# RetNet and mixture of depths in one kernel: the first batch's ranking, stores, loads and weights in another order

## The chip, the core and the metric

The kernel runs on one NeuronCore of a Trainium2 chip. The metric is the device time of one execution in microseconds (us). A core has a matrix engine (PE), a vector engine (DVE), a scalar engine (ACT), a general engine (POOL) and a queue processor (SP) that only issues transfers here; 16 DMA engines move data between memory and the on-chip SBUF. PE writes its results to PSUM.

## The reference

```
ret = ((q @ k^T) / 8 * gamma_h^(i-j) for j <= i) @ v     # 8 batches, 8 heads, 576 tokens, 64 wide
x = ret as (batch, 576, 512)
scores = x @ w_gate                                      # one number per token
top = the 128 tokens of a batch with the highest scores
out = x;  out[top] = x[top] + sigmoid(scores[top]) * (relu(x[top] @ w1) @ w2)   # w1 512x1024
```

Everything is float32. A token's rank in its batch is the number of tokens that score higher; tokens with rank below 128 go through the MLP.

## The kernel before, in words

A batch of 576 tokens is cut into 9 chunks of 64. A step of the main loop (line 487) handles two chunks, so there are 36 steps for 8 batches, and one more to finish; step 4 holds the last chunk of batch 0 and the first of batch 1. For each step one load of 1 MB brings q, k, v and a second layout of k (`load`, L108). POOL scales v with the decay (`scaled`, L189, tile `vs`). PE makes the products of q and k (`sc_ps`), the running state (`u_ps`, copied to `st` by ACT, L209), and, one step later, the output (`y_ps`). DVE applies the causal mask (`masked`, L262). `values` scales the output by the other decay: in the steps in `BUSY` by eight small ACT instructions (L272), in the others by one of DVE (L275); then two DVE instructions score the two chunks (L283). `stored` (L291 to L296) writes the output of a step in two transfers, or four where a step spans two batches.

When a batch, or a part of it (`cuts`), is scored, four functions rank it: `flatten` lays the scores on a diagonal, `spread` broadcasts them over the partitions by a matmul and an ACT copy, `compare` counts on DVE how many scores are higher than those of one block of 128 tokens (with a first instruction that picks the block's own scores), `one_hot` turns ranks into a selection. `fetch` makes token indices by a matmul and starts an indirect gather of 128 rows from memory on POOL (L375); the rows must have been stored before. `mlp` transposes them on PE (`turn`, tile `xg_ps`, L394) and puts eight parts into a list: four `up` (first layer, `h_ps`) and four `down` (second layer, `ye_ps`), 1.9 us of PE each. Each step takes some parts from the list so that they are used up by the next batch's turn. After the last `down`, POOL scatters the new rows (L419).

The order on each engine in `ENGINES` is the order in which the code emits instructions; POOL isn't in that set before, so a scheduler orders it. PE executes the matmuls of a step in an interleave of two streams; the plan `inner` puts a function at a place (step, i) inside it, `first` right after the matmuls, `soon` and `mid` after `values`, `late` and `then` at the step's end. Transfers are issued by SP in order. `pe` counts PE work and, about once a step, issues a due weight piece (a list `weights` with due steps) and the next load, both made to wait behind a matmul of that step. Each transfer also waits until the one eight places earlier on SP has landed.

```
load(); load()                        # start: table, loads 0 and 1, w_gate halves,
load(); load(); ...; load()           # loads 2 and 3, second table part, load 4
weights.append((5 + f // 2, ...))     # w1 pieces due in steps 5 to 8, w2 pieces in 9 to 12
```

Of the kernel before, what the change touches and what calls it, by code (L numbers as in the profile page):

```python
# [10 lines left out]
F32 = mybir.dt.float32  # L11
# [6 lines left out]
P = 128  # L18
# [3 lines left out]
BEFORE = 65  # L22
SURE = 8
ET = mybir.EngineType
ENGINES = {ET.PE, ET.DVE, ET.Activation, ET.SP}


def layout(NC, HG, cap):
# [11 lines left out]
def kernel(  # L40
# [22 lines left out]

    nc = tc.nc
    NS = qkvk.shape[0]
    DM = w1.shape[0]
    F = w1.shape[1]
    D = DM // H
    KD, FB = DM // P, F // P
    B = len(outs)  # L70
# [22 lines left out]

    raw, weights = {}, deque()
    now = {"at": BEFORE, "edge": BLOCK, "load": 0, "step": 0, "quiet": 0}

    def load(behind=None):
        s, now["load"] = now["load"], now["load"] + 1  # L100
# [4 lines left out]
                  qkvk[s, :, DM * a : DM * (a + n)].rearrange("p (a e) -> p a e", a=n), behind)  # L105

    def start(out, in_, behind):
        ins = nc.sync.dma_start(out=out, in_=in_)  # L108
        if behind is not None:
            tc.add_manual_dep(ins.ins, behind.ins.name, mybir.DependencyInfo(  # L110
                mybir.DependencyClass.Sync, mybir.DependencyReason.DATA), reason="behind a fetch")

    def pe(ins, n=4):

        now["at"] += n
        if now["at"] >= now["edge"] + SURE:
            now["edge"] += BLOCK
            lead = now["load"] - now["step"]
            if now["quiet"] and lead > 2:
                now["quiet"] -= 1  # L120
                return ins
            due = weights and weights[0][0] <= now["step"]
            if due:
                start(*weights.popleft()[1:], ins)
            if now["load"] < NS and lead < 4:
                load(ins)
        return ins
# [18 lines left out]
    for i, half in enumerate(halves):  # L146
        nc.sync.dma_start(out=wg_half[half, :], in_=spread_out(W * i, W, C))
    load()
    load()
    nc.sync.dma_start(out=table[:, n_first:], in_=consts[:, n_first:])  # L150
    load()
    w1_sb = const.tile([P, KD, F], F32, name="w1_sb")
    w2_sb = const.tile([P, FB, DM], F32, name="w2_sb")
    for f in range(0, FB, 2):
        e = slice(P * f, P * f + 2 * P)
        weights.append((5 + f // 2, w1_sb[:, :, e], w1[:, e].rearrange("(a p) f -> p a f", p=P)))
    for f in range(0, FB, 2):
        weights.append((9 + f // 2, w2_sb[:, f : f + 2, :],
                        w2[P * f : P * f + 2 * P, :].rearrange("(a p) d -> p a d", p=P)))

    dec = table[:, : 2 * (NC + 1) * HG].rearrange("p (s c h) -> p s c h", s=2, c=NC + 1)
    causal = table[:, col["causal"] : col["causal"] + C]
# [16 lines left out]

    BUSY = [s for s in range(1, (NC - 1) // 2 + 3) if s != (NC - 1) // 2]
    vs, am, sc_ps, y_ps, u_ps, st, xs, sc = {}, {}, {}, {}, {}, {}, {}, {}
    factor = lambda s, i: dec[:, i, chunk(s, 0)[1] : chunk(s, 0)[1] + 2, :].unsqueeze(3).to_broadcast(
        [P, 2, HG, D])

    def scaled(s):
        vs[s] = work.tile([P, DM], F32, name="vs")
        nc.gpsimd.tensor_tensor(out=four(vs[s]), in0=four(raw[s][:, 2, :]), in1=factor(s, 0),  # L189
                                op=OP.mult)  # L190

# [72 lines left out]
            in1=causal.unsqueeze(1).to_broadcast([P, H, C]), op=OP.mult)  # L264

    def values(s):
        xs[s] = work.tile([P, DM], F32, name="xs", bufs=5)
        if s in BUSY:
            c = chunk(s, 0)[1]
            for a in range(2):  # L270
                for h in range(HG):
                    nc.scalar.activation(out=xs[s][:, hd[a][h]], in_=y_ps[s][:, hd[a][h]],  # L272
                                         func=AF.Copy, scale=dec[:, 1, c + a, h : h + 1])
        else:
            nc.vector.tensor_tensor(out=four(xs[s]), in0=four(y_ps[s]), in1=factor(s, 1),  # L275
                                    op=OP.mult)
        for a in range(2):
            b, c = chunk(s, a)
            if c == 0:
                sc[b] = work.tile([P, NC], F32, name="sc", bufs=3)  # L280
            part = xs[s][:, W * a : W * a + W]
            scr = work.tile([P, DM], F32, name="scr", bufs=1)
            nc.vector.scalar_tensor_tensor(scr[:, :W], part, 1.0, wg_half, op0=OP.mult,  # L283
                                           op1=OP.mult, accum_out=sc[b][:, c : c + 1])

    def stored(s):
        (b, c), (b1, _) = chunk(s, 0), chunk(s, 1)
# [12 lines left out]
    flat, row, tok, rank, hot = {}, {}, {}, {}, {}  # L300

    EARLY = (2 * NC // 3) // 2 * 2
    cuts = lambda b: [0, EARLY, NC] if b in (0, B - 2, B - 1) else [0, NC]

    def flatten(b, part):

# [26 lines left out]
    def compare(b, j, part):  # L333


        if b not in rank:
            rank[b] = work.tile([P, 2, NJ], F32, name="rank", bufs=2)
            tok[b] = work.tile([P, NJ], F32, name="tok", bufs=2)
        scr = work.tile([P, S], F32, name="scr2", bufs=1)
        n = min(P, S - P * j)  # L340
        new = j in own(b, part)
        if new:
            nc.vector.scalar_tensor_tensor(  # L343
                scr[:, :n], row[b][:, P * j : P * j + n], 1.0, eye[:, :n], op0=OP.mult,
                op1=OP.mult, accum_out=tok[b][:, j : j + 1])
        i0, i1 = C * cuts(b)[part], C * cuts(b)[part + 1]
        if new:
            i0 = 0
        at = P * (NJ - 1 - j)
        nc.vector.scalar_tensor_tensor(  # L350
            scr[:, : i1 - i0], row[b][:, i0:i1], tok[b][:, j : j + 1], ahead[:, at + i0 : at + i1],
            op0=OP.subtract, op1=OP.is_gt, accum_out=rank[b][:, 0 if new else part, j : j + 1])
# [14 lines left out]
    def fetch(b):  # L367
        t = bank("idx_ps")
        for j in range(NJ):
            n = min(P, S - P * j)  # L370
            matmul(t[:, :1], hot[b][:n, j, :], place[:n, j : j + 1], start=j == 0, stop=j == NJ - 1)
        idx[b] = work.tile([P, 1], I32, name="idx", bufs=6)
        nc.scalar.copy(out=idx[b], in_=t[:, :1])
        xr[b] = work.tile([P, DM], F32, name="xr", bufs=6)
        nc.gpsimd.indirect_dma_start(  # L375
            out=xr[b], out_offset=None, in_=outs[b],
            in_offset=bass.IndirectOffsetOnAxis(ap=idx[b][:, :1], axis=0))
        now["quiet"] = int(b > 0)

    def gates(b):  # L380
        scr = work.tile([P, DM], F32, name="scr", bufs=1)
# [57 lines left out]
    for b in range(B):  # L439
        end = cuts(b)  # L440

        there = [(NC * b + c - 1) // 2 + 1 for c in end[1:]]
        last = len(there) - 1
        for part, s in enumerate(there):
            plan(soon, s, flatten, b, part)
        for part, s in enumerate(there[:-1]):
            plan(mid, s + 1, spread, b, part)
            for j in own(b, part):
                plan(then if b < B - 1 else mid, s + 1 + int(b == 0 and j > 1), compare, b, j, part)
        if b == B - 1:  # L450
            break
        s = there[-1]
        js = [*range(own(b, last).start), *own(b, last)]
        if b == 0:


            plan(inner, (s + 1, 12), spread, b, last)
            for j in js:
                plan(first, s + 1 + int(j > 2), compare, b, j, last)
            plan(first, s + 2, one_hot, b)  # L460
            plan(inner, (s + 3, 4), fetch, b)
            plan(inner, (s + 5, 4), mlp, b)
            plan(inner, (s + 5, 13), some, 1)
            ready.append(s + 5)
            plan(then, s + 5, gates, b)
            continue


        if last:
            when = 1, (1, 1, 1, 1, 2), 2, 3, 4  # L470
        elif b == 1:
            when = 1, (1, 1, 1, 2, 2), 2, 3, 4
        else:
            when = 1, (1, 1, 2, 2, 3), 3, 4, 5 + int(b > 2)
        plan(late, s + when[0], spread, b, last)
        for j in js:
            plan(then, s + when[1][min(j, 4)], compare, b, j, last)
        plan(then, s + when[2], one_hot, b)
        plan(mid, s + when[3], fetch, b)
        plan(late, s + when[4], mlp, b)  # L480
        ready.append(s + when[4] + 1)
        if b < B - 2:
            plan(then, s + when[4] + 1, gates, b)
    ready.append(NS + 1)

    scaled(0)
    for s in range(NS + 1):
        now["step"] = s
        now["at"] += 1.5
        if s == 1:  # L490
            nc.sync.dma_start(out=wg, in_=spread_out(0, DM, P))
        while now["load"] < min(NS, s + 2):
            load()
        if s + 1 < NS:
            scaled(s + 1)
        matmuls(s)
        if s > 1:
            stored(s - 2)
        for f, a in first.get(s, []):
            f(*a)  # L500
        if s:
            values(s - 1)
        if s == 1:
            nc.vector.tensor_copy(out=place, in_=table[:, col["place"] : col["end"]])
        for f, a in soon.get(s, []) + mid.get(s, []):
            f(*a)

        n = -(-len(parts) // max(1, min([r for r in ready if r > s], default=s + 1) - s))
        some(n if s < NS else len(parts) - 1)
        for f, a in late.get(s, []) + then.get(s, []):  # L510
            f(*a)
    stored(NS - 1)

    b, part = B - 1, len(cuts(B - 1)) - 2
# [73 lines left out]
```

## Time and profile before

| | |
|---|---|
| three runs, us | 258.15, 265.55, 264.25 (median 264.25) |
| the profiled execution, us | 259.76 |
| its span from first to last instruction, us | 258.1 |
| PE busy in the span | 225.4 us (87%) |
| DVE, ACT, POOL busy | 151.2, 59.3, 59.6 us |
| DMA: moved, mean rate | 56.95 MB, 221 GB/s |
| the first batch's transposes start | 53.41 us |

The profile comes from one execution. A line of the windows gives for one stretch of time how long each engine was busy; "PEclk" is the share of full clock that PE was granted; the DMA share is the mean busy share of the 16 DMA engines. PE's matmuls are pipelined, so a busy PE needn't be at its peak. The chain of waits follows the work that ended last back to what released it.

### The profile page before, as it was taken

The page shows a single profiled execution, that of the slowest core. Times are in us where ns is not written, and L with a number is a line of the kernel's source. Part 1 is how long each engine was busy: PE and PEld are TensorE (multiplying, and loading weights), DVE is VectorE, ACT ScalarE, POOL GpSimd, SP SyncE. Part 2 cuts the span into 40 slices and gives each one's busy share as a digit, 9 for nine tenths or more (in the row PEclk, how much of TensorE's full clock was granted, in tenths as well). Part 3 has the DMA queues.
Part 4 walks back from the last instruction along what each step waited for, and adds up shares of the span by engine and source line. Part 5 has one row for each costly group of instructions (what it writes and reads, how often), then busy time and mean ns, then how long its engine had stood idle before and what let it go on. Part 6 is the DMA issues. An engine that isn't in the chain of part 4 may idle for free.

```text
span 258.1 us, 11373 instructions
## 1 busy us (share of the span) xinstructions
PE 225.4 (87%) x5102; PEld 174.8 (68%) x5102; DVE 151.2 (59%) x436; ACT 59.3 (23%) x178; POOL 59.6 (23%) x59
## 2 busy tenths in 40 slices
PE   8565785689889989896999999999999999999991
PEld 3564574579755887555985799568966895784940
DVE  0156788542885536973983699579944861950201
ACT  1125443112510223112221321122211220211200
POOL 3333113312141112133131150413312210101101
PEclk9889979759999999999999999999999999999999
DMA  6999899998666776881778985888876303111101
GB/s 210 403 324 341 260 339 372 379 390 273 212 226 226 234 266 229 289 283 64 235 241 288 301 288 169 263 259 296 285 251 227 99 17 80 44 41 41 43 0 41
DMA packets 20945, 56.95 MB, mean 221 GB/s; under 512 B 2336, under 2 KB 13984, under 8 KB 16416
## 3 DMA queue, kind: packets, MB, share of 16 engines
q1 hardware_dynamic: 19616, 52.02, 59.9%
q0 software_dynamic: 1280, 4.20, 4.6%
q8 instruction: 40, 0.66, 1.0%
q14 instruction: 9, 0.07, 0.1%
HBM read 44.67 MB, written 11.53 MB: 218 GB/s over the span
## 4 chain that ended last, share of the span: by engine, by line
PE 51%; issue 24%; DMA 20%; POOL 2%; POOLq 1%; SPq 0%; DVE 0%
PE h_ps L134 14%; DMA raw<-in_qkvk 10%; PE ye_ps L134 9%; PE u_ps L134 8%; DMA xr<-out,idx 8%; PE sc_ps L134 8%; PE y_ps L134 7%; PE row_ps L134 3%; DMA w_sb<-in_w 2%; PE xg_ps L394 1%; POOL out L419 1%; POOL xr L375 1%; POOL vs L189 1%; POOLq L584 0%; SPq L108 0%
## 5 line engine op out<-in xcount | busy, mean ns | idle before, releaser
L189 POOL TENSOR_TENSOR vs<-raw,table 128x512 f32<-128x512 f32 x36 | 40.1, 1113 | 140.2 <-DMA raw<-in_qkvk 105.1
L134 PE MATMUL h_ps<-xg,w_sb 128*128 128x128 f32 x512 | 61.9, 280 | 0.1
L134 PEld LDWEIGHTS h_ps<-xg,w_sb 128*128 128x128 f32 x512 | 59.6, 195 | 2.2 <-issue 1.2
L134 PE MATMUL ye_ps<-w_sb,hT 128*128 128x512 f32 x128 | 60.1, 605 | 0.0
L134 PE MATMUL u_ps<-vs,raw 64*64 64x64 f32 x1024 | 45.9, 229 | 7.3 <-POOL vs L189 3.1
L262 DVE TENSOR_TENSOR am<-sc_ps,table 128x512 f32<-128x512 f32 x36 | 24.8, 688 | 45.5 <-PE sc_ps L134 26.5
L134 PE MATMUL y_ps<-vs,am 64*64 64x64 f32 x1152 | 46.1, 229 | 5.3 <-issue 4.8
L134 PEld LDWEIGHTS u_ps<-vs,raw 64*64 64x64 f32 x1024 | 37.8, 140 | 18.6 <-issue 12.8
L134 PE MATMUL sc_ps<-raw 64*64 64x64 f32 x1152 | 45.3, 228 | 4.4 <-issue 4.1
L134 PEld LDWEIGHTS sc_ps<-raw 64*64 64x64 f32 x1152 | 40.4, 143 | 9.2 <-issue 7.9
L209 ACT COPY st<-u_ps 128x256 f32<-128x256 f32 x64 | 24.0, 375 | 90.0 <-PE u_ps L134 59.9
L134 PEld LDWEIGHTS y_ps<-vs,am 64*64 64x64 f32 x1152 | 39.5, 141 | 5.4 <-issue 4.8
L134 PE MATMUL y_ps<-st,raw 64*64 64x64 f32 x1024 | 39.9, 226 | 0.9 <-issue 0.8
L283 DVE SCALAR_TENSOR_TENSOR scr<-xs,wg_half 128x256 f32<-128x256 f32 x72 | 34.8, 483 | 6.6 <-ACT xs L272 4.1
L350 DVE SCALAR_TENSOR_TENSOR scr<-row,tok,ahead 128x576 f32<-128x576 f32 (+2 forms) x49 | 36.2, 739 | 2.8 <-ACT row L326 0.8
L134 PEld LDWEIGHTS ye_ps<-w_sb,hT 128*128 128x128 f32 x128 | 22.7, 190 | 21.1 <-issue 20.1
L134 PEld LDWEIGHTS y_ps<-st,raw 64*64 64x64 f32 x1024 | 35.8, 141 | 1.3 <-issue 1.2
L275 DVE TENSOR_TENSOR xs<-y_ps,table 128x512 f32<-128x512 f32 x31 | 21.1, 682 | 7.4 <-PE y_ps L134 7.4
L406 ACT ACTIVATE hT<-h_ps 128x256 f32<-128x256 f32 x32 | 12.3, 384 | 49.1 <-PE h_ps L134 49.1
L343 DVE SCALAR_TENSOR_TENSOR scr<-row,table 128x128 f32<-128x128 f32 (+1 forms) x40 | 12.7, 317 | 14.9 <-ACT row L326 14.2
L418 DVE SCALAR_TENSOR_TENSOR o<-ye_ps,gate,xr 128x512 f32<-128x512 f32 x8 | 6.0, 750 | 24.4 <-issue 12.7
L419 POOL DMA_INDIRECT out<-o,idx x8 | 9.0, 1130 | 35.2 <-DVE o L418 32.5
(32 smaller groups left out, 106.2 us busy)
## 6 DMA issues: line engine op xcount, KB each, us to landing
raw<-in_qkvk SPq DMA_DIRECT2D x35, 1024.0 KB, 5.4
out<-xs SPq DMA_DIRECT2D x64, 128.0 KB, 5.5
w_sb<-in_w SPq DMA_DIRECT2D x8, 512.0 KB, 6.5
raw<-in_qkvk SPq DMA_DIRECT2D x2, 512.0 KB
out<-xs SPq DMA_DIRECT2D x16, 64.0 KB, 6.3
wg<-in_w_gate SPq DMA_DIRECT2D x1, 256.0 KB
table<-in_consts SPq DMA_DIRECT2D x1, 130.5 KB
wg_half<-in_w_gate SPq DMA_DIRECT2D x2, 64.0 KB, 7.3
```

The source lines that it names most:

```text
L134: return pe(nc.tensor.matmul(out, lhsT, rhs, **more), 4 if lhsT.dtype == F32 else 2)
L189: nc.gpsimd.tensor_tensor(out=four(vs[s]), in0=four(raw[s][:, 2, :]), in1=factor(s, 0), op=OP.mult)
L209: nc.scalar.copy(out=st[b, c], in_=u_ps[b][:, :W])
L262: nc.vector.tensor_tensor(out=am[s], in0=sc_ps[s].rearrange("p (h d) -> p h d", h=H), in1=causal.unsqueeze(1).to_broadcast([P, H, C]), op= ...
L275: nc.vector.tensor_tensor(out=four(xs[s]), in0=four(y_ps[s]), in1=factor(s, 1), op=OP.mult)
L283: nc.vector.scalar_tensor_tensor(scr[:, :W], part, 1.0, wg_half, op0=OP.mult, op1=OP.mult, accum_out=sc[b][:, c : c + 1])
L343: nc.vector.scalar_tensor_tensor(scr[:, :n], row[b][:, P * j : P * j + n], 1.0, eye[:, :n], op0=OP.mult, op1=OP.mult, accum_out=tok[b][:, ...
L350: nc.vector.scalar_tensor_tensor(scr[:, : i1 - i0], row[b][:, i0:i1], tok[b][:, j : j + 1], ahead[:, at + i0 : at + i1], op0=OP.subtract, ...
L375: nc.gpsimd.indirect_dma_start(out=xr[b], out_offset=None, in_=outs[b], in_offset=bass.IndirectOffsetOnAxis(ap=idx[b][:, :1], axis=0))
L406: nc.scalar.activation(out=hT[b][:, f : f + n, :], in_=t[:, :n, :], func=AF.Relu)
L418: nc.vector.scalar_tensor_tensor(o, ye[b], gate[b], xr[b], op0=OP.mult, op1=OP.add)
L419: nc.gpsimd.indirect_dma_start(out=outs[b], out_offset=bass.IndirectOffsetOnAxis(ap=idx[b][:, :1], axis=0), in_=o, in_offset=None)
```

## The change

- **Ranking of batch 0** in three parts of 4, 4 and 1 chunks instead of 6 and 3. The part of 1 chunk is scored first in step 5: DVE scales that half of the output and scores it at once, ACT scales the other half (step 4's output joins `BUSY`). Every part now compares the blocks before it too. Fetch moves from step 8 to step 7, the MLP from step 10 to step 9.
- **Stores and hold.** `stored` of steps 0 and 1 is emitted in step 4, of 2 and 3 in step 5, of 4 at the end of step 5; of 5 and 6 in step 9, 7 and 8 in step 10, 9 in step 11; from 12 on as before. From batch 0's fetch to the end of step 7's matmuls, loads and weights that would be issued are held and then issued behind a tiny memset on POOL after the gather.
- **Loads.** Three at the start, each later one behind a matmul one step later than before.
- **Weights** are due in steps 7, 8, 9, 9, 10, 10, 11, 12, up to two at a time after step 8; their layout in memory has a piece's row of 4 KB per partition in one run. `wg` is loaded in step 4.
- **POOL** is in `ENGINES`, so its order is the emitted one; `scaled` is emitted two steps ahead, at the step's end (four buffers for `vs`; nine for `xs`).
- **Later batches.** Fetch of batches 1 to 5 moves from the middle to the end of its step, the MLP of batches 1 and 2 one step later.

```diff
-ENGINES = {ET.PE, ET.DVE, ET.Activation, ET.SP}
+ENGINES = {ET.PE, ET.DVE, ET.Activation, ET.SP, ET.Pool}
...
     def start(out, in_, behind):
+        if behind is not None and now["hold"]:
+            held.append((out, in_))
+            return
...
-            due = weights and weights[0][0] <= now["step"]
-            if due:
-                start(*weights.popleft()[1:], ins)
+            for _ in range(1 + (now["step"] > 8)):
+                if weights and weights[0][0] <= now["step"]:
+                    start(*weights.popleft()[1:], ins)
...
     load()
-    load()
     nc.sync.dma_start(out=table[:, n_first:], in_=consts[:, n_first:])
-    load()
...
-        weights.append((5 + f // 2, w1_sb[:, :, e], w1[:, e].rearrange("(a p) f -> p a f", p=P)))
+    due = 7, 8, 9, 9, 10, 10, 11, 12
+        weights.append((due[i], w1_sb[:, :, e], w1[i].rearrange("p (a f) -> p a f", a=KD)))
...
-    BUSY = [s for s in range(1, (NC - 1) // 2 + 3) if s != (NC - 1) // 2]
+    BUSY = range(1, (NC - 1) // 2 + 3)
...
     def values(s):
+        if s == (NC - 1) // 2:
+            nc.vector.tensor_tensor(
+                out=xs[s][:, :W].rearrange("p (h d) -> p h d", h=HG),
+                in0=y_ps[s][:, :W].rearrange("p (h d) -> p h d", h=HG),
+                in1=dec[:, 1, c0, :].unsqueeze(2).to_broadcast([P, HG, D]), op=OP.mult)
+            scored(s, 0)
...
-    cuts = lambda b: [0, EARLY, NC] if b in (0, B - 2, B - 1) else [0, NC]
+    cuts = lambda b: [0, NC // 2, NC - 1, NC] if b == 0 else (
+        [0, EARLY, NC] if b >= B - 2 else [0, NC])
...
-        now["quiet"] = int(b > 0)
+        now["quiet"], now["hold"] = int(b > 0), int(b == 0)
...
-            plan(inner, (s + 1, 12), spread, b, last)
+            plan(inner, (s + 1, 7), spread, b, last)
             for j in js(last):
-                plan(first, s + 1 + int(j > 2), compare, b, j, last)
-            plan(first, s + 2, one_hot, b)
-            plan(inner, (s + 3, 4), fetch, b)
-            plan(inner, (s + 5, 4), mlp, b)
-            plan(inner, (s + 5, 13), some, 1)
-            ready.append(s + 5)
-            plan(then, s + 5, gates, b)
+                plan(first, s + 1, compare, b, j, last)
+            plan(first, s + 1, one_hot, b)
+            plan(inner, (s + 2, 5), fetch, b)
+            plan(inner, (s + 4, 6), mlp, b)
+            plan(inner, (s + 4, 15), some, 1)
+            ready.append(s + 4)
+            plan(then, s + 4, gates, b)
...
-            when = 1, (1, 1, 1, 2, 2), 2, 3, 4
+            when = 1, (1, 1, 1, 2, 2), 2, 3, 5
-            when = 1, (1, 1, 2, 2, 3), 3, 4, 5 + int(b > 2)
+            when = 1, (1, 1, 2, 2, 3), 3, 4, 6
-        plan(mid, s + when[3], fetch, b)
+        plan(mid if last else late, s + when[3], fetch, b)
...
+    FETCH = (NC - 1) // 2 + 3
+    stores = {4: [0, 1], 5: [2, 3], 6: [], FETCH: [], FETCH + 1: [], FETCH + 2: [5, 6],
+              FETCH + 3: [7, 8], FETCH + 4: [9]}
+    tick = const.tile([P, 1], F32, name="tick")
...
-        if s + 1 < NS:
-            scaled(s + 1)
         matmuls(s)
-        if s > 1:
-            stored(s - 2)
+        if s == FETCH:
+            now["hold"], ins = 0, nc.gpsimd.memset(tick, 0.0)
+            while held:
+                start(*held.popleft(), ins)
+        for r in stores.get(s, [s - 2] if s > FETCH + 4 else []):
+            stored(r)
...
+        if s == (NC - 1) // 2 + 1:
+            for f, a in then.pop(s):
+                f(*a)
+            scored(s - 1, 1)
+            stored(s - 1)
...
+        if s + 2 < NS:
+            scaled(s + 2)
```

## The prediction

> **What bounds the kernel now.** I read the engine shares first, then stages, then the chain of waits inside the stages that lose time.
>
> The page and the windows by stage (columns: stage, its length, then busy us of PE, PEld, DVE, ACT, POOL, granted clock, DMA share, GB/s):
>
> ```profile
> span 258.1 us, 11373 instructions
> DMA  6999899998666776881778985888876303111101
> 20.00:30.00 10.00, 5.90 (x263) 4.87 (x266) 5.97 (x18) 5.49 (x24) 2.44 (x3) 1.00 0.98 315
> 40.00:50.00 10.00, 5.33 (x235) 4.64 (x231) 7.17 (x21) 2.83 (x12) 3.60 (x4) 0.94 1.03 384
> 50.00:60.00 10.00, 8.71 (x162) 7.71 (x155) 5.86 (x15) 1.29 (x4) 1.88 (x2) 0.55 1.00 370
> 60.00:70.00 10.00, 9.32 (x193) 8.56 (x192) 4.54 (x13) 4.38 (x10) 1.55 (x2) 1.00 0.66 220
> 70.00:80.00 10.00, 8.89 (x224) 5.29 (x226) 6.70 (x21) 1.29 (x4) 2.60 (x2) 1.00 0.79 263
> 80.00:90.00 10.00, 9.41 (x198) 7.55 (x191) 7.02 (x16) 2.09 (x5) 2.08 (x2) 1.00 0.65 203
> 90.00:100.00 10.00, 9.17 (x281) 8.36 (x283) 3.63 (x12) 3.15 (x9) 2.07 (x2) 1.00 0.73 254
> 100.00:120.00 20.00, 15.89 (x412) 10.19 (x401) 14.87 (x43) 3.08 (x9) 6.74 (x6) 1.00 0.71 239
> 150.00:200.00 50.00, 49.41 (x1150) 38.50 (x1152) 37.82 (x111) 10.91 (x31) 14.13 (x13) 1.00 0.77 258
> ```
>
> Three stages. Until about 53 us the DMA engines are full and PE has little to do; from 120 to 230 us PE is full; between them PE loses 7.3 us (60 us less 9.32+8.89+9.41+9.17+15.89). Nothing in the first stage gains unless the first batch's MLP, which is what fills PE, starts earlier or steps arrive faster.
>
> The timeline of POOL (start, us, instruction, idle before it):
>
> ```profile
> 19.32 1.04 POOL L189 TENSOR_TENSOR vs<-raw,table 128x512 f32<-128x512 f32 x1 [2.97 <-DMA raw<-in_qkvk]
> 43.88 1.04 POOL L189 TENSOR_TENSOR vs<-raw,table 128x512 f32<-128x512 f32 x1 [3.49 <-DMA raw<-in_qkvk]
> 45.41 1.14 POOL L375 DMA_INDIRECT xr<-out,idx  x1 [0.49 <-DMA w_sb<-in_w]
> 111.75 1.57 POOL L189 TENSOR_TENSOR vs<-raw,table 128x512 f32<-128x512 f32 x1 [5.37 <-DMA raw<-in_qkvk]
> 113.47 0.99 POOL L375 DMA_INDIRECT xr<-out,idx  x1 [0.15 <-DMA raw<-in_qkvk]
> ```
>
> `vs` of step s starts when load s has landed, so these starts are a clock of the loads: from step 4 (19.32) to step 9 (43.88) 24.56 us, 4.9 us a step. A step then moves one load of 1.05 MB, a store of 0.26 and a weight piece of 0.52: 1.83 MB / 4.9 us = 374 GB/s. The DMA is the limit there.
>
> The chain of waits (start, us, what):
>
> ```profile
> 45.41 7.96 DMA xr<-out,idx
> 53.41 1.12 PE xg_ps L394 x4
> ...
> 107.89 5.54 DMA raw<-in_qkvk
> 113.42 0.05 issue
> 113.47 5.10 DMA xr<-out,idx
> 118.62 0.66 PE xg_ps L394 x4
> ```
>
> The first MLP begins at T = 53.41 us, with its gather on the chain. The third gather (113.47) stood on POOL behind a `vs` that waited for a load issued at 107.89. POOL isn't in the hand-written order before, so later `vs` came ahead of the gather.
>
> **What the skill says.** "DMA: Bandwidth & Descriptors", section "Issuing engines are not separate DMA queues": transfers of all issuers run on the same 16 DMA engines and interleave. The trace agrees: the eight gathers took 3.3 to 8.0 us to land, the longest the first, amid loads and weights. "TensorE: Matmul & The Clock Gate", section "What's actually happening": an idle window of about 3.4 us halves PE's clock. The trace agrees: granted clock 0.55 in 50 to 60 us, after PE stood. "GPSIMD Engine Reference", section "1. Specifications": GpSimd shares SBUF interfaces with VectorE when a VectorE instruction reads two SBUF inputs. Here the 128x256 scoring took 0.97 us at 19.67 beside `vs` at 19.32, and 0.43 us next after; `vs` instructions keep their number, so I price that move at nothing, with bounds of -0.5 to +0.5 us a step in the first ten steps.
>
> **The change, part by part.** Write P(s) for PE's start on step s.
>
> *Loads.* Five at the start become three; load s+2 instead of s+3 is issued behind the first matmuls of step s. The row of loads says 5.4 us from issue to landing. So: landing, `vs` 1.04 us, about 0.3 until SP is released, 0.35 to issue, 5.4 to land, 7.1 us for two steps, 3.6 us a step. By bytes (1.05 + 0.26 MB at 374 GB/s) it is 3.5 us. Both replace 4.9 us. P(1) = 9.92 + 1.04 = 11.0 and P(2) = 13.8, as before; load 3, issued at 11.2, lands at 16.6, P(3) = 17.8; then 3.6 each: P(5) = 25.0, P(6) = 28.6, P(7) = 32.2.
>
> *Ranking in 4, 4, 1.* After chunk 8 only a 64-wide compare for each of four blocks, one full block and the one-hot remain. Rows of before: 0.46 us for 128x192, 1.2 for a new block with its token column, 0.16 and 0.82 at the end; DVE in steps 5 and 6 sums to about 5.3 + 4.5 us, so `hot` is ready near 36 and the index near 36.5. PE, in order, stands at the fetch in step 7 meanwhile; it would wait for load 8 anyway, so I price that at zero (3 us if load 8 came early).
>
> *Stores and hold.* Eight store DMAs (steps 2 to 4 of the first batch) stand on SP ahead of load 8; an issue cost 0.5 to 1.5 us before, and the last also waits until the DMA eight places earlier, load 7 (landed near 31), is done. So load 8 is issued at 31.2 rather than 28.7, and shares with 1 MB of stores: landing 37.5 (bounds 36 to 41). On POOL the gather is behind `vs` 8: issued at 38.7. Loads and weights held go out behind the small memset after it, at 40: a 0.52 MB weight, then load 9. Gather 0.7 + weight 1.4 + load 5.4 = 7.5 us: landing 48.2, `vs` to 49.3, and 24 matmul calls of step 9 on a cold PE, 1.5 us: T = 50.8 against 53.4. The gather has landed by then. Gain 2.6; but at T PE has 9.4 steps done instead of 10.25, 0.85 x 2.1 us (a step took 2.1 us at 153 us) = 1.8 us more ahead. Net gain 0.8. With the bounds of load 8, -2.7 to +2.3.
>
> *POOL order, later fetches and MLPs.* Fetch 2 moves after step 18's MLP part, its MLP from step 19 to 20; MLP 1 from 13 to 14; no `vs` of a later step stands before a gather. A gather has a step or more (4 to 6 us) beyond its 5.0 us. Of the 7.3 us lost in 60 to 120 us I take 2.0 to remain (waits on ACT's state copies and issue). Gain 5.3, between 2 and 7.
>
> *Later weights.* MLP 0 spreads over steps 9 to 14, four of them with 3.95 us of PE (2.1 + one part, 1.9). From 41 us, DMA must move 8 weights 4.2, loads 9 to 15 7.3, seven stores 1.8 and two gathers 0.5: 13.9 MB, which PE's sums (step 9 9 us with its cold start, 10 6.9, then 3.95 to 4.7) want by about 81 us: 350 GB/s. The rows of 20 to 60 us average near 345: I add 0.7 us of stalls. Weight layout with whole 4 KB rows at the source: zero to -1 us. The lead of two loads costs nothing at 5.9 us a step (8.2 us from issue to scaled at a step's pace of 11.8 for two), and 0.3 us if a landing takes 8.0. The `wg` load (step 4 instead of 1), the one extra add and the split scaling of one step (0.4 us DVE for 0.9 us ACT) lie beside the loads: zero. Nothing changes from step 33 on, where PE is full, and the last scatter's tail stays.
>
> *Sum.* 0.8 + 5.3 - 0.7 = 5.4 us, plus 0.5 for the weight rows: 5.9. The profiled execution took 259.76 us (span 258.1 and 1.7 around it): 253.9. The three runs shown have a median of 264.25, 4.5 above the profiled one, and lie from 258.15 to 265.55; the changed kernel has fewer waits of the kind that vary, so I name 254.0 and leave the upper scatter to the range.
>
> **Rivals.** *Nothing to measure:* the store burst and the hold give back what lighter steps gain. Load 8 issued at 36 (eight issues at 1.5 us from 24) puts T at 55.6: -2.2 - 1.8 + 5.3 - 0.7 + 0.5 = +1.1, 258.7. For it: pairs of issues took up to 3.03 us at 41 us. Against: many pairs took 1.26. *More gain:* 1 us of stalls is left in the middle and T is 47 (load 8 at 28.7, fewer bytes ahead of it): 6.4 - 1.8 + 6.3 + 0.5 = 11.4, 248.4. For it: in 4 to 16 us, with loads alone, the DMA moved 387 to 418 GB/s. Against: SP issues in order, the stores first. *Slower:* the deferred weights make the middle DMA-bound. Place: SP's queue from 41 to 85 us, where two or three transfers wait together behind one matmul and the stores and the next step's load stand behind them. Price: 13.9 MB at 265 GB/s take 52.5 us instead of 40, 12.5 us less 0.7 counted, 11.8 us on 253.9: 265.7. It cancels the gain at about 300 GB/s (46.3 us) and is 2% slower below 270 (51.5 us). For it: rates of 264 and 299 GB/s in 24 to 32 us, where stores mix in, at a busy share near 0.9. Against: 381 to 402 GB/s in 40 to 56 us, with the same mix. *The change isn't done:* excluded, the instruction order shows the parts as described.
>
> **Chances.** Forecast 0.52, nothing to measure 0.18, more gain 0.12, slower 0.18. About 2% is what can be told from no change here. Faster takes the second's none, and most of the first: 0.60; same 0.21; slower 0.19. The range 246 to 264 takes in the bounds of load 8 (5 us), of the middle (5 us) and the rival without change, and leaves out most of the slower one.
>
> **What would show it.** First transposes at 48 to 53 us; `vs` starts 3.6 us apart in steps 3 to 7; the gather on POOL right after `vs` 8 near 39; no gather on the chain after 60 us; PE idle below 3.5 us in 60 to 120 us. Wrong if `vs` starts in 55 to 85 us lag PE (loads late), or the first transposes come after 56 us.

## The result, and the profile after

The changed kernel takes 269.74 us (median of four runs, 268.28 to 273.12), the kernel before 262.02 us in the runs beside it (258.15 to 265.55): a ratio of 1.040, 95% interval 1.029 to 1.051. It is slower; the forecast was 254.0 us with a range of 246 to 264. The profiled execution of the change is the longest of its four (273.12 us), the ratios here leave the longer runs of a kernel out, and so a ratio need not be the quotient of two medians.

The page of the changed kernel, and its windows (columns as before: stage, length, busy us of PE, PEld, DVE, ACT, POOL, granted clock, DMA share, GB/s):

```profile
span 271.4 us, 11381 instructions
10.00:20.00 10.00, 7.22 (x256) 6.74 (x256) 2.99 (x8) 2.89 (x12) 2.09 (x3) 0.66 0.64 224
20.00:30.00 10.00, 6.05 (x274) 5.13 (x274) 6.87 (x25) 5.43 (x24) 3.27 (x3) 1.00 0.84 275
40.00:50.00 10.00, 6.38 (x245) 5.87 (x245) 6.45 (x24) 3.04 (x13) 2.71 (x4) 0.66 0.50 162
50.00:60.00 10.00, 3.13 (x74) 2.68 (x77) 1.16 (x5) 0.86 (x2) 1.36 (x2) 0.73 0.79 298
70.00:80.00 10.00, 9.16 (x273) 7.29 (x274) 6.10 (x21) 2.68 (x7) 1.67 (x2) 1.00 1.04 414
80.00:90.00 10.00, 8.20 (x151) 5.33 (x144) 6.59 (x19) 0.90 (x3) 3.08 (x3) 0.77 0.99 357
```

The stage that was full of transfers no longer is: 224 GB/s in 10 to 20 us and 162 GB/s in 40 to 50 us, where the kernel before moved 353 and 384. The loads are not slower for it. From issue to `vs`, loads 5 to 9 took 5.8 to 8.9 us in the kernel before (mean 7.6) and 4.9 to 8.2 us in the changed one (mean 6.6). They were issued later.

POOL's timeline, in the form shown for the kernel before, where `vs` is the clock of the loads (`vs` of steps 2, 3, 8, the gather, the memset that lets the held transfers go, `vs` of step 9):

```profile
13.57 1.04 POOL L192 TENSOR_TENSOR vs<-raw,table 128x512 f32<-128x512 f32 x1 [1.73 <-DMA raw<-in_qkvk]
20.00 1.19 POOL L192 TENSOR_TENSOR vs<-raw,table 128x512 f32<-128x512 f32 x1 [5.39 <-DMA raw<-in_qkvk]
...
45.10 1.04 POOL L192 TENSOR_TENSOR vs<-raw,table 128x512 f32<-128x512 f32 x1 [4.69 <-DMA raw<-in_qkvk]
46.31 1.13 POOL L389 DMA_INDIRECT xr<-out,idx  x1 [0.17 <-issue]
47.45 0.12 POOL L519 MEMSET tick<- 128x1 f32 x1
55.78 1.04 POOL L192 TENSOR_TENSOR vs<-raw,table 128x512 f32<-128x512 f32 x1 [8.21 <-DMA raw<-in_qkvk]
```

From step 3 to step 8 it is 25.1 us, 5.0 a step. In the kernel before the same two starts are these, 24.0 us apart, 4.8 a step:

```profile
15.31 1.04 POOL L189 TENSOR_TENSOR vs<-raw,table 128x512 f32<-128x512 f32 x1 [1.51 <-DMA raw<-in_qkvk]
...
39.34 1.04 POOL L189 TENSOR_TENSOR vs<-raw,table 128x512 f32<-128x512 f32 x1 [4.79 <-DMA raw<-in_qkvk]
```

So the changed kernel is 4.7 us behind at step 3 and 5.8 us at step 8, where lighter steps were to put it ahead. The chain of waits runs through these loads:

```profile
13.05 6.88 DMA raw<-in_qkvk
...
29.93 0.43 DVE flat L325
30.40 0.98 PE row_ps L137 x2
...
32.27 6.89 DMA raw<-in_qkvk
39.18 0.47 SPq L309
39.75 5.19 DMA raw<-in_qkvk
...
46.31 1.13 POOL xr L389
...
48.26 7.35 DMA raw<-in_qkvk
...
58.43 1.04 PE xg_ps L408 x4
```

Read from the top: load 3 is issued at 13.05 us and is at work 6.9 us later. Load 7 is issued only at 32.27 us: its matmul of step 5 stands behind `row_ps`, the broadcast of the ranking, and that waited for DVE's `flat`. Load 8 leaves SP at 39.75 us, behind the last of eight stores (39.18), and that store stood eight places after load 7 and waited for it to land. Load 9 was held for the gather and leaves at 48.26 us. The first transposes start at T = 58.43 us (53.41 before).

What each stage got done shows in PE's busy time times the granted clock, in us at full clock. The product is rough, since both are means over a window. The last two kernels are experiments described below.

| | before | changed | `lead3` | `mid_nohold` |
|---|---|---|---|---|
| 0 to 60 us | 41.36 x 0.86 = 35.6 | 36.58 x 0.81 = 29.6 | 41.36 x 0.86 = 35.6 | 43.12 x 0.86 = 37.1 |
| 60 to 120 us | 52.67 x 1.00 = 52.7 | 55.45 x 0.93 = 51.6 | 53.00 x 0.97 = 51.4 | 55.52 x 1.00 = 55.5 |
| 120 to 200 us | 79.41 x 1.00 = 79.4 | 75.32 x 1.00 = 75.3 | 75.26 x 1.00 = 75.3 | 76.22 x 1.00 = 76.2 |
| sum to 200 us | 167.7 | 156.5 | 162.3 | 168.8 |

At 200 us the changed kernel is 11.2 us of work behind: 6.0 from the first 60 us, 1.1 from the middle, 4.1 from 120 to 200 us, a stretch for which I had no term at all. After that little is lost: the sixth batch's transposes start 13.1 us later than before (212.05 against 199.00), and the two spans differ by 13.3. These are the lines of 120 to 200 us, of the kernel before and of the changed one:

```profile
120.00:200.00 80.00, 79.41 (x1985) 62.42 (x1987) 60.27 (x172) 18.78 (x53) 20.55 (x19) 1.00 0.76 251
```

```profile
120.00:200.00 80.00, 75.32 (x1807) 60.10 (x1810) 57.95 (x163) 18.23 (x51) 19.08 (x18) 1.00 0.74 241
```

Of the 4.7 us in which PE stands there (80 less 75.32), about 2.0 lie beside indirect transfers on POOL (0.5 in the kernel before), 0.7 is one gap for which the profile gives no reason, and 1.9 are two waits for `vs` of steps 20 and 21, whose loads had been issued 8.4 and 8.6 us before that `vs`:

```profile
125.31 0.27 PE L137 MATMUL u_ps<-vs,raw 64*64 64x64 f32 x2 [1.00 <-POOL vs L192]
130.64 0.27 PE L137 MATMUL u_ps<-vs,raw 64*64 64x64 f32 x2 [0.88 <-POOL vs L192]
```

In the middle PE is idle less, 4.55 us (60 less 55.45) against 7.33, but the clock took it back. The timeline of PE in the changed kernel, one group of four matmuls before, and one after a wait of 1.11 us ahead of the last index matmul of the second fetch (further gaps beside its gather are left out):

```profile
80.33 1.98 PE L137 MATMUL ye_ps<-w_sb,hT 128*128 128x512 f32 x4
...
83.80 0.16 PE L137 MATMUL idx_ps<-place,hot 64*128 64x1 f16 x1 [1.11 <-issue]
...
88.09 3.78 PE L137 MATMUL ye_ps<-w_sb,hT 128*128 128x512 f32 x4
```

The four matmuls take 3.78 us in place of 1.98, and the granted clock is 0.50 from 86 to 92 us. "TensorE: Matmul & The Clock Gate" in the Trainium skill, section "What's actually happening", says that an idle window of some 3.4 us brings half clock. Here no such window was wholly idle: PE was busy 2.20 of the 4 us from 82 to 86. The kernel before shows the same ahead of its half clock in 50 to 60 us, with PE busy 1.80 of the 3.4 us from 45.5 to 48.9. But a half idle stretch does not always bring it: in 20 to 30 us PE was busy 6.05 of 10 us at full clock. What decides is not shown.

### The profile page after: what moved, and what is told of

It reads as the page before. It is cut to its first block, busy times and chain, and to the rows that moved or that the text cites. A ratio compares the mean times of both kernels' runs of the same rounds, so it can differ in the third digit from the quotient of the medians.

```text
span 271.4 us, 11381 instructions
## 1 busy us (share of the span) xinstructions
PE 231.8 (85%) x5104; PEld 179.1 (66%) x5104; DVE 150.9 (56%) x444; ACT 60.7 (22%) x183; POOL 58.2 (21%) x60
## 4 chain that ended last, share of the span: by engine, by line
PE 49%; issue 22%; DMA 16%; DVE 5%; POOL 4%; ACT 2%; SPq 1%; POOLq 1%; DVEq 0%
DMA raw<-in_qkvk 16%; PE h_ps L137 14%; PE ye_ps L137 12%; PE u_ps L137 7%; PE sc_ps L137 7%; PE y_ps L137 6%; POOL vs L192 2%; PE row_ps L137 2%; DVE scr L364 2%; POOL xr L389 1%; PE xg_ps L408 1%; DVE scr L296 1%; DVE scr L357 1%; ACT xs L281 1%; SPq L111 1%
## 5 line engine op out<-in xcount | busy, mean ns | idle before, releaser
L192 POOL TENSOR_TENSOR vs<-raw,table 128x512 f32<-128x512 f32 x36 | 38.8, 1078 | 132.7 <-DMA raw<-in_qkvk 106.4
L137 PE MATMUL u_ps<-vs,raw 64*64 64x64 f32 x1024 | 47.6, 236 | 22.6 <-POOL vs L192 19.9
L137 PE MATMUL ye_ps<-w_sb,hT 128*128 128x512 f32 x128 | 62.0, 620 | 0.0
L137 PEld LDWEIGHTS u_ps<-vs,raw 64*64 64x64 f32 x1024 | 39.7, 148 | 32.3 <-POOL vs L192 22.5
L137 PE MATMUL h_ps<-xg,w_sb 128*128 128x128 f32 x512 | 60.8, 277 | 0.0
L137 PE MATMUL y_ps<-vs,am 64*64 64x64 f32 x1152 | 49.6, 234 | 1.7 <-issue 1.2
L137 PE MATMUL sc_ps<-raw 64*64 64x64 f32 x1152 | 47.9, 231 | 2.4 <-issue 2.0
L137 PEld LDWEIGHTS sc_ps<-raw 64*64 64x64 f32 x1152 | 42.1, 145 | 7.5 <-issue 5.6
L137 PEld LDWEIGHTS y_ps<-vs,am 64*64 64x64 f32 x1152 | 41.8, 145 | 3.8 <-issue 2.8
L364 DVE SCALAR_TENSOR_TENSOR scr<-row,tok,ahead 128x576 f32<-128x576 f32 (+5 forms) x52 | 38.1, 732 | 2.7 <-ACT xg L409 0.5
L137 PEld LDWEIGHTS y_ps<-st,raw 64*64 64x64 f32 x1024 | 37.1, 146 | 1.8 <-issue 1.8
L296 DVE SCALAR_TENSOR_TENSOR scr<-xs,wg_half 128x256 f32<-128x256 f32 x72 | 32.7, 454 | 7.1 <-ACT xs L281 4.8
L432 DVE SCALAR_TENSOR_TENSOR o<-ye_ps,gate,xr 128x512 f32<-128x512 f32 x8 | 6.0, 748 | 26.1 <-PE ye_ps L137 13.3
L357 DVE SCALAR_TENSOR_TENSOR scr<-row,table 128x128 f32<-128x128 f32 (+1 forms) x40 | 13.8, 346 | 9.9 <-ACT row L340 9.2
L433 POOL DMA_INDIRECT out<-o,idx x8 | 8.6, 1072 | 48.2 <-DVE o L432 34.8
```

The costliest lines, as they stand in the source:

```text
L137: return pe(nc.tensor.matmul(out, lhsT, rhs, **more), 4 if lhsT.dtype == F32 else 2)
L357: nc.vector.scalar_tensor_tensor(scr[:, :n], row[b][:, P * j : P * j + n], 1.0, eye[:, :n], op0=OP.mult, op1=OP.mult, accum_out=tok[b][:, ...
L364: nc.vector.scalar_tensor_tensor(scr[:, : i1 - i0], row[b][:, i0:i1], tok[b][:, j : j + 1], ahead[:, at + i0 : at + i1], op0=OP.subtract, ...
L432: nc.vector.scalar_tensor_tensor(o, ye[b], gate[b], xr[b], op0=OP.mult, op1=OP.add)
L433: nc.gpsimd.indirect_dma_start(out=outs[b], out_offset=bass.IndirectOffsetOnAxis(ap=idx[b][:, :1], axis=0), in_=o, in_offset=None)
```

## The experiments

Runs are compared with runs of the kernel before on the same chip. Each expectation says itself what its theories give.

| kernel | median us (lowest to highest) | kernel before, median | ratio, 95% interval |
|---|---|---|---|
| `lead3` | 264.42 (258.08 to 269.42) | 261.90 | 1.000 (0.994 to 1.006) |
| `start5_lead2` | 271.79 (270.32 to 273.82) | 261.90 | 1.040 (1.032 to 1.048) |
| `before_lead2` | 268.67 (265.54 to 272.21) | 261.90 | 1.030 (1.020 to 1.040) |
| `catchup` | 268.69 (266.38 to 269.32) | 261.90 | 1.031 (1.023 to 1.038) |
| `lead3_mid` | 262.17 (258.00 to 269.97) | 262.68 | 0.997 (0.991 to 1.002) |
| `before_pool` | 264.38 (257.94 to 266.52) | 262.68 | none given |
| `gath_attn` | 269.88 (266.95 to 272.67) | 262.68 | 1.029 (1.017 to 1.042) |
| `gath_mlp` | 266.34 (264.51 to 272.56) | 262.68 | 1.020 (1.008 to 1.031) |
| `gath_late2` | 280.08 (277.32 to 281.80) | 262.93 | 1.081 (1.064 to 1.098) |
| `gath_mid2` | 270.49 (270.16 to 273.83) | 262.93 | 1.052 (1.034 to 1.069) |
| `after_nohold` | 265.29 (259.78 to 268.03) | 262.93 | 1.013 (0.982 to 1.045) |
| `mid_nohold` | 261.11 (260.04 to 262.82) | 262.93 | 1.013 (1.001 to 1.026) |

### How far ahead the loads run

`lead3` is the changed kernel with five loads at the start, as before; each load up to number 15 is then one step further ahead too. Later the lead evens out. After each fetch of a later batch `pe` leaves out one load where three are ahead, and from load 22 on every kernel here issues load s+2 in step s.

```diff
     load()
+    load()
     nc.sync.dma_start(out=table[:, n_first:], in_=consts[:, n_first:])
+    load()
```

> The changed kernel with five loads at the start instead of three, so that load s+3 again is issued in step s; nothing else undone. Theory A (two loads in flight cannot fill the DMA; a load took 6.9 us from issue to scaling with nothing else queued): vs of steps 3 to 7 come back to 15 to 33 us, the first transposes start at 49 to 52 us instead of 58.4, the time is 252 to 258. Theory B (the eight stores and the hold in front of load 9 cost it): the first transposes stay at 55 us or later and the time at 264 to 270.

The kernel came back to 264.42 us, 5.3 us below the changed one. Its ratio to the kernel before is 1.000; the medians of all 20 and 23 runs are 2.5 us apart, so some of the loss may be left. The transposes moved as theory A has it, the time fell short of its 252 to 258. POOL's timeline, `vs` of steps 3 and 8:

```profile
16.22 1.25 POOL L194 TENSOR_TENSOR vs<-raw,table 128x512 f32<-128x512 f32 x1 [1.50 <-DMA raw<-in_qkvk]
...
38.84 1.10 POOL L194 TENSOR_TENSOR vs<-raw,table 128x512 f32<-128x512 f32 x1 [5.02 <-DMA raw<-in_qkvk]
```

That is 4.5 us a step, and T is 51.2 us. The other side of the same test puts three loads into the kernel before:

```diff
     load()
-    load()
     nc.sync.dma_start(out=table[:, n_first:], in_=consts[:, n_first:])
-    load()
```

> The kernel before with three loads at the start instead of five and nothing else: load s+2 is issued in step s. Theory A: 266 to 274, vs of step 3 near 20 us, and the first transposes at 58 us or later. Theory B: within 2% of the kernel before, 259 to 266.

It costs 6.8 us (268.67 against 261.90), with T at 60.8 us instead of 53.4, though `vs` 3 came at 17.8 us and not near 20. In the kernel before, too, the lead of three is worth its keep. Is it the first two loads of the start, or the lead that they give to all later ones? `start5_lead2` has five at the start and then falls back to a lead of two, since the next load is issued only when fewer than three are ahead:

```diff
-            if now["load"] < NS and lead < 4:
+            if now["load"] < NS and lead < 3:
```

> The changed kernel with five loads at the start, but the pace held to load s+2 from step 3 on. It parts the start from the pace. If the slow start alone costs (one empty stretch of the DMA between 12 and 14 us): the time is within 2 us of lead3. If the pace costs: 264 to 268, between lead3 and the changed kernel, with transposes at 54 us or later.

It takes 271.79 us. Its timeline has `vs` of steps 3 and 4 as early as `lead3`, and then the gap, at step 5:

```profile
16.11 1.04 POOL L194 TENSOR_TENSOR vs<-raw,table 128x512 f32<-128x512 f32 x1 [1.48 <-DMA raw<-in_qkvk]
19.48 1.05 POOL L194 TENSOR_TENSOR vs<-raw,table 128x512 f32<-128x512 f32 x1 [2.33 <-DMA raw<-in_qkvk]
27.85 1.04 POOL L194 TENSOR_TENSOR vs<-raw,table 128x512 f32<-128x512 f32 x1 [7.33 <-DMA raw<-in_qkvk]
```

T is 59.0 us, and the time is above the 264 to 268 that I had named for a cost of the pace. So the early start by itself gains nothing: once the lead falls to two, the steps come late, and from step 5 to step 8 they are 5.8 us apart (`vs` 8 at 45.31) against 5.0 in `lead3`. `catchup` gives the changed kernel its third load of lead later, in step 13:

```diff
+            if now["step"] == 13:
+                load(ins)
```

> The changed kernel with one extra load in step 13, so that load s+3 is issued in step s from there on; the start is untouched. If the short lead also costs in the later stage, where PE waits a little in every step: 4 to 8 us faster than the changed kernel. If only the first 60 us cost: within 2 us of it.

It takes 268.69 us, about 1 us less than the changed kernel. The lead is three for loads 16 and 18 to 21 (18 to 21 in `lead3`), and then evens out here too. PE has no wait for `vs` in its 120 to 200 us, where the changed kernel had 1.9 us. The lead matters where the loads bind, before the first MLP, and little after it. Its T was 54.9 us although its code up to step 13 is that of the changed kernel, so T itself moves by some 3.5 us from one execution to another, and single values of T can't carry a small difference.

### The hold

```diff
-        now["quiet"], now["hold"] = int(b > 0), int(b == 0)
+        now["quiet"], now["hold"] = int(b > 0), 0
```

> The changed kernel with nothing held around the first gather: load 9 and the weight are issued behind PE's step 7 as others are. If the hold is part of the late start: load 9 is issued near 44 us instead of 48.3, the first transposes come 3 to 4 us earlier, 2 to 4 us faster than the changed kernel. Rival (without the hold the gather is slowed by the load, which takes as much): within 1 us.

265.29 us, 4.4 us below the changed kernel by the medians, with an interval that doesn't separate it from either side (0.982 to 1.045). In the trace the gather starts at 45.23 us and `vs` 9 at 50.54 instead of 55.78 us; T is 53.0 us. Load 9 no longer has to wait for the gather, and the first MLP begins sooner. From `vs` 8 to T it takes 8.9 us here, against 13.3 to 13.8 in the three traces with the hold and a lead of two there (the changed kernel, `start5_lead2`, `catchup`), so the hold costs about 4.5 us at this place. Nothing in this trace shows a gather so slowed by the transfers beside it that the hold would be worth its wait.

### Where POOL's gathers stand

`lead3` still lost 4 us in 120 to 200 us. Of PE's 4.7 us of idle time there, about 2.4 lie beside indirect transfers, 1.7 is one wait for `vs` at 181.31 us, and 0.7 one gap without a reason in the profile. In the trace of the changed kernel PE shows two gaps where POOL executes an indirect transfer beside the attention's products of 64x64. POOL's and PE's timelines of the changed kernel, one of the gathers moved to the end of a step:

```profile
143.78 0.99 POOL L389 DMA_INDIRECT xr<-out,idx  x1 [3.77 <-ACT idx L387]
```

```profile
144.36 0.26 PE L137 MATMUL y_ps<-vs,am 64*64 64x64 f32 x1 [0.17 <-issue]
145.10 0.21 PE L137 MATMUL sc_ps<-raw 64*64 64x64 f32 x1 [0.41 <-issue]
```

Counted over the starts of PE's matmuls against their usual spacing, such a gather or scatter costs 0.5 to 1.0 us. After 60 us, 9 of the changed kernel's 15 indirect transfers fall there (five gathers, four scatters), and 3 of 15 before, all scatters: moving `fetch` behind the MLP part of its step puts the gather beside the next step's attention. The first test undoes that move alone on `lead3`, except for batch 1, whose fetch keeps the place after the part:

```diff
-        plan(mid if last else late, s + when[3], fetch, b)
+        plan(late if b == 1 else mid, s + when[3], fetch, b)
```

> The kernel lead3 with the fetch of batches 2 to 5 back in the middle of its step, ahead of the MLP part, as in the kernel before; nothing else undone. Theory C: four gathers leave the attention matmuls, 2 to 4 us faster than lead3. Rival (the place of the fetch is hidden): within 1 us of lead3, or slower where PE then waits for the one-hot.

262.17 us, 2.2 us below `lead3`, whose runs were on another chip. In the trace four of the indirect transfers lose PE time beside the attention now, one gather and three scatters. The earlier place has a price as well: PE now waits for a ranking, and half clock follows.

```profile
120.00:140.00 20.00, 17.24 (x426) 16.58 (x424) 13.06 (x35) 3.86 (x11) 5.71 (x5) 0.83 0.68 219
...
131.19 0.38 PE L137 MATMUL idx_ps<-place,hot 128*128 128x1 f16 x5 [2.76 <-DVE hot L376]
```

The sign is right; the difference is of the order of the scatter. Two attempts to make the cost larger added 16 gathers whose result nobody uses:

```diff
...
         state(s, a)
+        if a == 0 and 17 <= s < 33:
+            extra()
...
```

> The kernel lead3 with 16 extra gathers of 128 rows (their result is not used), one in each of steps 17 to 32, each released by ACT in the middle of that step's small attention matmuls. Theory C (while POOL executes an indirect DMA, PE loses about 0.9 us of a stretch of 64x64 matmuls, as the trace of the changed kernel shows at ten places): 10 to 16 us slower than lead3. Rival (the gaps there are PE's instruction fetch or DMA traffic, and only stand beside the gathers): within 4 us of lead3, and the same as gath_mlp.

```diff
-        if a == 0 and 17 <= s < 33:
-            extra()
...
         n = 1 if s == FETCH + 2 else n
+        if 17 <= s < 33:
+            extra()
```

> The same 16 extra gathers, each released after the step's attention matmuls, where PE has MLP matmuls of 0.12 or 0.48 us. Theory C: within 4 us of lead3, at least 8 us faster than gath_attn. If the extra traffic or POOL's time costs: as slow as gath_attn.

269.88 and 266.34 us. This pair failed as a test: the traces show that the first one's gathers, released by ACT after a state copy, mostly ran beside the end of the attention or the MLP's matmuls, where neither kernel loses more than 0.3 us, so the difference of 3.5 us says little. In the trace of `gath_attn` a single wait of 3.5 us, ahead of the output's matmuls at 161.97 us, with half clock after it, is as large. One gather of the second that did meet the attention, at 183.57 us, cost 0.66 us. The next pair makes each extra gather wait for PE as a true fetch does, with five matmuls and an ACT copy before it, after the MLP part of twelve steps or before it:

```diff
         some(n if s < NS else len(parts) - 1)
+        if s in (17, 19, 20, 21, 23, 24, 25, 26, 28, 29, 30, 32):
+            extra()
```

> In gath_attn most extra gathers ran beside the end of a step's attention or beside MLP matmuls, so it did not test theory C. Here the kernel lead3 gets 12 extra gathers (result unused) in steps 17 to 32, each with the five index matmuls and the ACT cast of a real fetch, all placed after the step's MLP part as the changed kernel places its fetches, so that POOL executes them beside the next step's sc and y matmuls. Theory C: 12 times 0.8 us of PE stalls and 12 times 0.3 us of index matmuls, about 13 us slower than lead3, 8 to 12 us slower than gath_mid2, and an excess near 0.8 us beside each. Rival (what stalls PE there isn't the gather): no more than 4 us from lead3 and from gath_mid2.

```diff
+        if s in (17, 19, 20, 21, 23, 24, 25, 26, 28, 29, 30, 32):
+            extra()
         some(n if s < NS else len(parts) - 1)
-        if s in (17, 19, 20, 21, 23, 24, 25, 26, 28, 29, 30, 32):
-            extra()
```

> The same 12 extra fetches placed before the step's MLP part. Theory C: 3 to 5 us slower than lead3, from the index matmuls alone, no stall beside the extra gathers. Rival: as gath_late2.

280.08 against 270.49 us. The same instructions cost 9.6 us more when they stand after the part, 0.8 us for each of the twelve. The trace of `gath_mid2` has both cases within 4 us; first POOL, then PE. The gather at 135.65 us is a true fetch, after the part; the one at 138.98 us is an extra one, before it:

```profile
135.65 0.98 POOL L405 DMA_INDIRECT xr<-out,idx  x1 [4.81 <-ACT idx L403]
136.66 1.05 POOL L194 TENSOR_TENSOR vs<-raw,table 128x512 f32<-128x512 f32 x1
138.98 0.98 POOL L393 DMA_INDIRECT xd<-out,i  x1 [1.27 <-ACT i L391]
```

```profile
136.23 0.21 PE L137 MATMUL y_ps<-vs,am 64*64 64x64 f32 x1 [0.16 <-issue]
...
136.95 0.21 PE L137 MATMUL sc_ps<-raw 64*64 64x64 f32 x1 [0.38 <-issue]
...
138.40 1.55 PE L137 MATMUL ye_ps<-w_sb,hT 128*128 128x512 f32 x3
```

PE stands twice beside the first, not at all beside the second. In `gath_late2` eight or nine of the twelve met the attention, 0.75 to 1.02 us each; in `gath_mid2` eleven of twelve cost nothing. `gath_mid2` is still 6 us above `lead3`, whose runs were on another chip, more than the 3 to 5 I had expected for the extra work itself. That the two coincide and that the place decides is shown; why PE stands is not. The `vs` that follows a gather on POOL at once also runs there, but PE's gaps lie within the gather's own 1.0 us and just after it.

### POOL's order alone

```diff
-ENGINES = {ET.PE, ET.DVE, ET.Activation, ET.SP}
+ENGINES = {ET.PE, ET.DVE, ET.Activation, ET.SP, ET.Pool}
```

> The kernel before with POOL put into the hand-written order and nothing else: the second gather no longer stands behind the scaling of step 14, nor the third behind that of step 20. As the prediction has it: PE's 2.9 us before the third transposes and some of the waits near 83 us go, 2 to 4 us faster. Rival (the gathers then meet the attention matmuls, theory C, or POOL's order blocks scaling behind scatters): same or slower.

264.38 us against 262.68: no gain is shown, where 2 to 4 us were expected. The trace shows the mechanism that I had predicted: the third gather goes out ahead of the later `vs`, and PE's wait at the third transposes shrinks from 2.87 to 0.76 us. Whether those 2 us reached the end can't be told from four runs that lie between 257.94 and 266.52 us.

### Both parts undone

`mid_nohold` is `lead3_mid` without the hold, by the line shown above.

> The best combination so far: five loads at the start, fetch of batches 2 to 5 in the middle, no hold. It could beat the kernel before: 255 to 260. If the hold hides nothing once three loads are in flight: as lead3_mid, 260 to 263.

261.11 us by the median, 1.1 below `lead3_mid` and 1.8 below the kernel before; but the ratio is 1.013 (1.001 to 1.026), so it is not shown to beat it. Its windows tell where the rest goes:

```profile
100.00:120.00 20.00, 18.87 (x606) 13.40 (x609) 18.72 (x45) 4.91 (x13) 5.51 (x5) 1.00 0.73 242
120.00:140.00 20.00, 17.24 (x407) 14.50 (x402) 13.93 (x35) 3.42 (x11) 5.96 (x6) 1.00 0.76 240
```

It reaches 120 us with 4.3 us more work done than the kernel before (37.1 + 55.5 less 35.6 + 52.7), and gives 3.2 back by 200 us. PE's timeline names most of it, in one wait:

```profile
129.37 0.36 PE L137 MATMUL idx_ps<-place,hot 128*128 128x1 f16 x5 [2.76 <-DVE hot L376]
```

The kernel before runs the same matmuls at 133.79 us without a wait. A PE that is early meets a ranking that isn't early enough: DVE was busy 18.72 of the 20 us from 100 to 120 us, and 9.12 of the 9.40 us from there to the end of the wait. The clock stayed at 1.00 here, where the same wait of 2.76 us in `lead3_mid` was followed by half clock. Whether that ranking can be made earlier was not tried.

## Why the prediction was wrong

The failed step is *Loads*, with "The lead of two loads costs nothing" beside it: load 8 was issued 8.6 us later than predicted, and giving the third load of lead back made the kernel 5.3 us faster. A second is *POOL order, later fetches and MLPs*, which counted only what the new places gain.

- **Loads: "7.1 us for two steps, 3.6 us a step".** From step 3 to step 5 this came true, 7.1 us (20.00 to 27.08). Yet load 8 left at 39.75 us instead of 31.2, 8.6 us late, and the chain says where.
  - First, `vs` 3 started at 20.0 instead of 16.6. Load 3 was to be issued at 11.2 us "behind the first matmuls"; it waits for about the fourteenth call, on a PE at half clock, left at 13.05 and took 6.9 us for 5.4. This part varies: `vs` 3 was at 17.6 in `catchup` and 18.7 in `after_nohold`, with the same code up to there.
  - Second, the next issues hang on PE's order: from `vs` of a step to the issue behind that step's matmul I had 1.7 us. Step 4 had 1.73 (23.29 to 25.02), but step 5 took 5.2 (27.08 to 32.27; 4.5 and 5.8 in `catchup` and `after_nohold`), since a broadcast of the ranking now stands among those matmuls. That made load 7 another 3.5 us late.
  - Third, load 7 took 6.9 us to land instead of 5.4, and load 8 stood on SP behind a store that waited for it. The 5.4 us was the page's row, a median of the eight landings that the profile could time, only one of them before 90 us, at 8.5; in the stage that counted, loads 5 to 9 of the kernel before took 5.8 to 8.9 us from issue to `vs`.

  The ranking was put on the loads' path, and with a lead of two nothing was left to hide it. Restoring the lead of three gave 5.3 us in the changed kernel; taking it from the kernel before cost 6.8.
- **Stores and hold.** The eight stores took SP from 32.71 to 39.65 us, and the last did wait for load 7, as I had said; load 8 landed at 45.1 us instead of 37.5, outside the bounds that I gave (36 to 41), by what the loads above had lost. From there on the total held: 13.3 us from load 8 to T predicted (37.5 to 50.8), 13.3 measured (45.10 to 58.43). Part of that is luck. The 7.5 us that I added from 40 end at 47.5, not at the 48.2 that I wrote; the 8.2 us that this makes is what passed from the end of the memset (47.57) to `vs` 9 (55.78), since load 9 left 0.7 us after the memset, behind a weight, and then took 7.5 us. The hold adds its wait to load 9 however late load 8 is: without it, `vs` 8 to T is 8.9 us. What it costs at the end is not fixed, since the median 4.4 us lower comes with an interval too wide.
- **Ranking: `hot` near 36 us.** It was ready at 43.4, and 43.6 before: no gain from 4, 4, 1 in the changed kernel. Its chain starts when step 4 is scaled and scored, and that waits for the loads. In the seven traces with a lead of three it was ready at 41.1 to 42.9, a gain of 0.7 to 2.5 us where I had over 7. In `lead3` (42.9) load 8 was at work 6 us earlier than in the changed kernel: there DVE's compares are the path, and PE stood 2.8 us at the fetch behind them. That PE "would wait for load 8 anyway" was right for the changed kernel only; the 3 us that I gave for an early load 8 is what `lead3` shows.
- **Later fetches: gain 5.3 us.** PE's idle time in 60 to 120 us fell by 2.8, not 5.3, and the clock, 0.93 for 1.00, took 0.07 x 60 = 4.2 us. I had no line for the clock outside the cold start. I had also read the trace of the kernel before as an agreement with an idle window of 3.4 us, though PE was busy for half of the one ahead of its half clock; that shorter waits can do it was there to be seen. Nor had I a line for the gathers' place: nine meetings with the attention in place of three, 0.5 to 1.0 us each. No row of the page shows that; it takes a look at PE's gaps beside POOL's instructions, and the kernel before held three examples, as at 84.22 and 175.47 us.
- **Later weights: -0.7 us.** About right: with 414 and 357 GB/s from 70 to 90 us the transfers held PE up once in that stretch, 0.8 us at 78.26. The rival that ended on the slower side, a middle bound by these transfers, gave 265.7 us; the sign came true, its mechanism didn't. From 40 to 60 us the DMA moved too little (162 and 298 GB/s), with loads issued late, and not too much.
- **"Nothing changes from step 33 on"** holds for the code, but 4 us had been lost by then. "The lead of two loads costs nothing" failed in this stretch too, by the 1.9 us of waits for `vs` of steps 20 and 21.
- **The signs that I named.** T after 56 us was my mark for being wrong, and it came. Of the others, `vs` at 3.6 us and PE idle below 3.5 us failed; the gather right behind `vs` 8 came true. No gather's transfer is on the chain after 60 us, but the POOL instruction of the last two gathers is (224.37 and 245.89 us), as it was in the kernel before.

The medians, read in a row: 269.7 changed, 264.4 with the lead restored, 262.2 with the fetches put back as well, 261.1 without the hold; the kernel before lies at 261.9 to 262.9 on the chips used. The first step is shown twice, by adding and by removing; the second lies within the scatter by itself, and its cause is shown by the pair with twelve added gathers; the third is within the scatter. That the lead's cost in the changed kernel goes through the broadcasts is read from the chain; no run moved them alone. What stays open is why the parts that remain in `mid_nohold`, with POOL's order among them, gain nothing at the end.

## What to carry to other kernels

A landing time belongs to the stage in which it was measured, and it is only part of what a prefetch hides: before taking one off, write down behind which matmul each load is issued and what else stands before that matmul. When an instruction moves to another place in its step, look at what the other engines do at that place, not only at who waits for it. A stage that is made faster hands its gain to the next wait, here the ranking on DVE, so name that wait before the gain is counted.

## What was not expected of the hardware

- While POOL executed an indirect transfer (1.0 us), a dense stream of 64x64 matmuls lost 0.5 to 1.0 us, mostly in two gaps; 128x128 matmuls and those with 512 columns lost nothing. Twelve moved gathers: 9.6 us.
- Load 3, 1 MB issued when little but the end of load 2 was in flight, took 6.9 us from issue to use in the changed kernel, and 6.7, 5.5 and 5.2 in `after_nohold`, `before_lead2` and `catchup`. In 10 to 20 us the changed kernel moved 224 GB/s with one or two loads in flight, the kernel before 353 GB/s with more.
- Half clock came after 4 us in which PE was still busy 55% of the time, and lasted about 7 us. The same wait of 2.76 us brought it in `lead3_mid` and did not in `mid_nohold`.
